# Squared-ReLU activations of two transformer layers: rectified in place, squared two tiles at a time, with a new table of pace settings

## The chip, the cores and the metric

The kernel runs on one core of a Trainium2 chip. A core has five engines that work side by side and are synchronised by semaphores: TensorE (PE; matmuls, results in the PSUM banks), VectorE (DVE), ScalarE (ACT; here nearly only exponentials), GpSimd (POOL) and SyncE (SP; here it issues DMAs). The metric is the device time of one execution in microseconds (us), as the median of several runs; lower is better.

## What is computed

Two transformer layers on 2048 rows of 448 numbers (bfloat16), with the same weights: attention of 16 heads (28 wide) and a feed-forward network (FFN) with 1792 hidden units, whose activation is a squared ReLU.

```python
def _A_ref(x, wqkv, wo):                      # attention
    ...
    scores = jnp.einsum("bhqd,bhkd->bhqk", q, k) * scale
    p = _softmax(scores, axis=-1)
    o = jnp.einsum("bhqk,bhkd->bhqd", p, v)
    return (lambda x, *d: x.transpose(*d))(o, 0, 2, 1, 3).reshape(B, S, D) @ wo

def _B_ref(x, w1, b1, w2, b2):                # FFN
    h = jnp.einsum("bsd,df->bsf", x, w1) + b1
    zero = jnp.zeros_like(h)
    r = jnp.where(h > zero, h, zero)
    h = r * r
    out = jnp.einsum("bsf,fd->bsd", h, w2) + b2
    return out

x = A_x
x = x + _A_ref(_layernorm(x, axis=-1), A_wqkv, A_wo)
x = x + _B_ref(_layernorm(x, axis=-1), B_w1, B_b1, B_w2, B_b2)
x = x + _A_ref(_layernorm(x, axis=-1), A_wqkv, A_wo)
x = x + _B_ref(_layernorm(x, axis=-1), B_w1, B_b1, B_w2, B_b2)
```

## The kernel before

**Tiling.** Everything stays in SBUF between the layers. The rows go in blocks of 256 (`nt` = 2 tiles of 128): eight in layer 0; seven in layer 1, and then two of 128 rows. Heads are held in four groups `g` of four heads, each head padded to 32 rows, so that four heads fill 128 partitions. One *score tile* is 512 columns of transposed scores in one PSUM bank: for a block of 256 rows, one head and two tiles of keys. There are 1024 of them in each layer.

**The order is written at build time.** A planner (`Planner`, `run`) simulates the engines' clocks with a cost for each operation and lays down, one operation after the other, what each engine's instruction queue holds. Streams of operations compete by start time and by priority; the chip then executes the queues in that order. So a cost or a setting in the planner acts only through the order and the choices that it makes.

**Groups.** `s_stream` issues the score matmuls in groups of three score tiles (line 1154); `gi` is the number of the group, 683 in all. ScalarE turns a group into exponentials with one instruction (line 1192). ScalarE's share of a group can be cut to two tiles: then `apart` has picked a third tile for VectorE, and `a_unit` (line 1216 or 1214) and its followers compute its exponential there with integer arithmetic on the bits, sharing steps with GpSimd (`a_rest`, lines 1263 to 1278) or on VectorE alone (`a_whole`, lines 1232 to 1239; chosen when GpSimd's backlog is over `PLIM`). `apart` allows a tile when VectorE's load over the last `SPAN` us is at most `BUSY` (or `LOW`, when the FFN work is behind its track) and its backlog at most `TB` (or `TB2`). Groups listed in `FORCE` get a tile without these two tests, groups in `SKIP` get none.

**Pace.** The settings are module variables, and `PACE` maps a group's number to settings that hold from that group on (`globals().update(PACE.get(gi, {}))`).

**The values.** `p_stream` multiplies the exponentials with V (lines 1380 and 1345), `CHUNK` key tiles at a time. Then come normalisation, the output projection and the layer norm.

**The FFN** of a block is made in `chain`: the matmuls with `w1` (`mm_tile`, line 809) fill a PSUM tile of 512 columns, which is two chunks of 128 hidden units for a block of 256 rows, so seven tiles a block; for a block of 128 rows four chunks and four tiles. VectorE rectifies each tile into a buffer `r` (line 1584; two such buffers, `R_r`), and squares it from there into its place (line 1591), which `hidden` finds: parts of `K_sb[1]`, `Q_sb` and `V_sb[1]` that are no longer needed, and a tile `h`, in layer 0; `V_sb[0]` in layer 1. When the score groups are at an end, ScalarE takes some of these (lines 1582, 1589). Products with `w2` follow, and wait for the block's last square. `add_to_x` adds the result to `x_sb` (line 1513).

**Fillers.** To keep TensorE occupied, `s_stream` may repeat a group's score matmuls (up to `MORE` times), and `heat` puts in products whose result isn't used, when TensorE's load over `WINDOW` is below `HEAT`.

Of the kernel before, what the change touches and what calls it, by code (L numbers as in the profile page):

```python
# [38 lines left out]
XMIN = 4  # L39
HELD = 0.14  # L40
# [42 lines left out]
HTURNS = 3  # L83
C_PRIO = 1.6
# [65 lines left out]
PACE = {  # L150
    0: {'BUSY': 0.95, 'LOW': 0.7, 'CHUNK': 1, 'EV': 2.9, 'FAR': 6, 'KEEP': 5, 'LAG': 8, 'LEAD': 18, 'MARGIN': 3,
         'MORE': 3, 'PRE': 0.5, 'SLACK': 0.7, 'SPAN': 8, 'TB': 2.4, 'TB2': 2.4, 'V_AGE': 5, 'V_LAST': 3, 'V_PAST':
         2, 'C_PRIO': 1.6, 'V_PRIO': 4, 'V_LATE': 2.6, 'V_WAIT': 5, 'ASIDE': 1, 'XMIN': 4, 'HOLD': 6, 'LADD': 0.05,
         'RES': 2, 'RES2': 2, 'TASIDE': -0.2, 'EPRIO': 2.6, 'SPARE': 0, 'NEAR': 3, 'SOON': 1, 'VGAP': 0.03, 'PWAIT':
         0.3, 'PNEAR': 0.2, 'PORTP': 1, 'PLIM': 99.0},
    8: {'LEAD': 12, 'BUSY': 0.9, 'PLIM': 2},
    16: {'SPAN': 11},
    24: {'LAG': 3},
    32: {'PLIM': 2.6, 'EV': 3.5},
    40: {'TB2': 3.0},  # L160
    42: {'BUSY': 0.95, 'CHUNK': 3, 'EV': 2.9, 'LAG': 8, 'LEAD': 18, 'MORE': 1, 'SPAN': 8, 'TB': 1.6, 'TB2': 2.4,
         'V_PRIO': 8.5},
    56: {'BUSY': 1.0, 'LAG': 3},
    64: {'NEAR': 9, 'ASIDE': 0.2, 'LADD': 0.1},
    72: {'V_AGE': 4},
    88: {'V_AGE': 3},
    112: {'C_PRIO': 1.2, 'HOLD': 5},
    120: {'LEAD': 10, 'LAG': 12, 'SPARE': 3, 'ASIDE': 2},
    128: {'TB': 2.0, 'MORE': 3},
    136: {'PRE': 1.2, 'MARGIN': 6},  # L170
    144: {'EPRIO': 4},
    152: {'CHUNK': 1, 'VGAP': 0},
    160: {'BUSY': 0.95, 'V_PRIO': 4, 'V_PAST': 3},
    168: {'RES': 1, 'C_PRIO': 2.1, 'LOW': 1.0},
    176: {'EV': 2.2, 'TB2': 2.0, 'LOW': 0.5},
    192: {'PORTP': 0.3, 'SOON': 0.6},
    200: {'CHUNK': 2, 'PRE': 0.3},
    208: {'PNEAR': 0.25, 'V_AGE': 6},
    216: {'NEAR': 3},
    248: {'EPRIO': 6},  # L180
    256: {'ASIDE': 0},
    264: {'MARGIN': 10},
    280: {'PORTP': 2},
    288: {'HOLD': 6},
    296: {'TB': 1.0, 'PNEAR': 0.15},
    304: {'SPAN': 6},
    312: {'BUSY': 1.0},
    320: {'LEAD': 12, 'MARGIN': 6},
    328: {'V_LATE': 6},
    336: {'LOW': 1.0},  # L190
    360: {'PNEAR': 0.05, 'TB': 2.4, 'V_LATE': 2.6, 'V_AGE': 3},
    368: {'C_PRIO': 1.6},
    376: {'PNEAR': 0.15, 'V_PRIO': 8.5},
    384: {'XMIN': 3, 'LEAD': 18},
    392: {'CHUNK': 3},
    400: {'KEEP': 6, 'ASIDE': 4, 'V_AGE': 6, 'BUSY': 0.9},
    408: {'PWAIT': 0.6, 'MORE': 1},
    424: {'RES': 2, 'BUSY': 1.0},
    440: {'HEAT': 0.6, 'WINDOW': 3.4, 'CHUNK': 2},
    456: {'V_AGE': 5, 'TB': 1.3},  # L200
    480: {'TB': 1.6, 'PORTP': 0.3, 'PLIM': 2},
    488: {'LADD': 0.2, 'HOLD': 4},
    496: {'MARGIN': 3, 'PNEAR': 0.35},
    504: {'PWAIT': 0.3},
    512: {'KEEP': 4, 'EV': 2.9},
    520: {'V_AGE': 4, 'C_PRIO': 1.2, 'HOLD': 5},
    528: {'PRE': 0.8},
    536: {'XMIN': 4, 'SPAN': 15, 'ASIDE': 2, 'PRE': 0.3},
    544: {'V_AGE': 5, 'EV': 2.2},
    552: {'PORTP': 1, 'LEAD': 12, 'FAR': 17, 'PRE': 0},  # L210
    560: {'V_LATE': 6, 'VGAP': 0.03},
    568: {'SPARE': 0, 'NEAR': 9},
    576: {'SOON': 1.5, 'PNEAR': 0.15},
    584: {'PLIM': 1.3, 'LAG': 3, 'V_WAIT': 3},
    592: {'KEEP': 6, 'V_LAST': 2.2},
    600: {'V_AGE': 8},
    608: {'EV': 1.3, 'LOW': 0.8},
    616: {'PRE': 1.2, 'BUSY': 0.95, 'V_PAST': 2, 'FAR': 6},
    624: {'LADD': 0.1, 'BUSY': 0.9},
    648: {'PRE': 0.5, 'SPAN': 20, 'EV': 3.5, 'ASIDE': 0.2},  # L220
    656: {'ASIDE': 1, 'SLACK': 0.4},
    672: {'SOON': 1, 'ASIDE': 0.2},
    680: {'SLACK': 0.7},
# [183 lines left out]
def kernel(  # L407
# [45 lines left out]
    R_r, R_xt, R_os, R_xn, R_on, R_rec = Res(2), Res(2), Res(NOS), Res(2), Res(2), Res(2)  # L453
# [31 lines left out]
    def flat_of(t):  # L485
        return t[:, :, :].rearrange("p g s -> p (g s)")
# [63 lines left out]
    def loads():  # L550
# [28 lines left out]
        yield dma(b2w[0:1, :], B_b2.rearrange("(o d) -> o d", o=1), 30 * kb, ("b2",))  # L579
# [937 lines left out]
    def chain(l, qb):  # L1517
# [30 lines left out]
        if late:  # L1548
            b2b = flat_of(K_sb[0])[:, S:S + D]
            if ("b2b",) not in pl.tok:  # L1550
# [11 lines left out]
        def hidden(i):  # L1562
            flat = lambda a: a.rearrange("p (f q) -> p f q", q=n)
            if l == 0 and i < 4:
                return (K_sb[1], Q_sb)[i // 2][:, 2 * (i % 2):2 * (i % 2) + 2, t0 * P:t0 * P + n]
            if l == 0 and i < 6:
                return flat(V_sb[1][:, t0:t0 + nt, :, :].rearrange("p t h r -> p (t h r)")[:, QB * (i - 4):QB * (i - 3)])
# [4 lines left out]
            return flat(V_sb[0][:, :, :, :].rearrange("p t h r -> p (t h r)")[:, c:c + QB])  # L1572
        for f0 in range(0, NFC, pack):
            fcs = range(f0, min(f0 + pack, NFC))
            w = len(fcs) * n
            split = late > 2 - THALF and f0 == 0
            b = {}

            def relu(e, t, b=b, w=w):
                r = b["r"] = rp.tile([P, QB], DT.bfloat16, name="r")  # L1580
                if e == "ACT":
                    nc.scalar.activation(out=r[:, 0:w], in_=t[:, 0:w], func=AF.Relu)  # L1582
                else:
                    nc.vector.tensor_scalar(out=r[:, 0:w], in0=t[:, 0:w], scalar1=0.0, scalar2=None, op0=ALU.max)  # L1584
            def square(e, b=b, w=w, f0=f0):
                r = b["r"][:, 0:w].rearrange("p (f q) -> p f q", q=n)
                b["h"] = h = hidden(f0 // pack)
                if e == "ACT":
                    nc.scalar.activation(out=h[:, 0:w // n, :], in_=r, func=AF.Square)
                else:  # L1590
                    nc.vector.tensor_tensor(out=h[:, 0:w // n, :], in0=r, in1=r, op=ALU.mult)  # L1591

            def then(o, b=b, square=square):
# [3 lines left out]
            o = yield from mm_tile(  # L1597
                [(i * n, n, [(w1[:, dc, fc * P:(fc + 1) * P], xnT[:, dc, 0:n], *([ends[dc // 2]] if split else [])) for dc in range(NDC)])
                 for i, fc in enumerate(fcs)],
                relu, 0.685, [*([] if split else ends), ("w1",)], True, post=[then], acq=R_r, across=split)  # L1600
            done[l] += w / 512
            for i in range(len(fcs)):
                hacts.append((b, i, b["s"]))
        yield Op("DVE", 0.0, None, deps=[o], rel=own_xt)
        mv = moments()
        for j in range(nt):
# [21 lines left out]
    def heat():  # L1628


        for gi in itertools.count(HFROM):
# [3 lines left out]
            for turn in range(HTURNS):  # L1635
                if HEAT <= pl.load(WINDOW) or not s_left or len(units) - at[0] < HSTOP:
                    break
# [57 lines left out]
```

## Time and profile before

| | us |
|---|---|
| median of 3 runs (803.57 to 803.78) | 803.65 |
| the profiled execution's own time | 803.48 |
| its span, from the first to the last instruction | 801.7 |

A row of the page's fifth part reads: line, engine, operation, output and inputs with shapes, count | busy us, mean ns of one | idle time of the engine before them, and what ended most of it. A row of stretches reads: start and end, length, then the busy us of each engine with its count of instructions, the granted TensorE clock, the DMA share and GB/s. Matmul ends are modelled, and a busy PE is not PE at its peak.

### The profile page before, as it was taken

Reading aid. Unit: us, or ns where it says so; the run is one execution under the profiler, and the core shown is the slowest. Engines: PE = TensorE matmul, PEld = TensorE weight load, DVE = VectorE, ACT = ScalarE, POOL = GpSimd, SP = SyncE. Lnnn points to the kernel's source line nnn. Section 1 sums busy time; section 2 is a strip of 40 time slices with the busy share of each in tenths; the row PEclk is TensorE's granted clock in tenths of the full one; section 3 lists DMA queues with packets and bytes.
Section 4 is the critical chain, followed back from the end, with each engine's and each line's share of the span. In section 5 each row is a group of like instructions: output and inputs, shape, how many; then the busy total and the mean of one; then the engine's idle time right before and its main releaser. Section 6 shows DMA issues by size and latency. Waiting matters only on the chain.

```text
span 801.7 us, 29246 instructions
## 1 busy us (share of the span) xinstructions
PE 778.7 (97%) x12242; PEld 417.6 (52%) x12242; DVE 744.8 (93%) x1818; ACT 789.4 (98%) x702; POOL 454.7 (57%) x717
## 2 busy tenths in 40 slices
PE   9999989999999999999999999989999999999998
PEld 6555545544555545555455545445454544545666
DVE  8999999999999999999999998999999999989564
ACT  8999999999999999999999999999999999999995
POOL 3346777657676664544566657657665566654200
PEclk9999999999999999999999999999999999999999
DMA  9300010000000000000000000011100000000100
GB/s 250 86 2 2 5 34 23 17 16 16 17 3 16 16 16 16 3 16 15 2 3 2 3 2 2 15 32 30 33 11 22 21 28 21 22 23 9 27 8 19
DMA packets 32480, 18.13 MB, mean 23 GB/s; under 512 B 17818, under 2 KB 31899, under 8 KB 32348
## 3 DMA queue, kind: packets, MB, share of 16 engines
q1 hardware_dynamic: 32204, 16.16, 7.4%
q8 instruction: 95, 1.56, 0.8%
q14 instruction: 37, 0.30, 0.1%
q10 hardware_dynamic: 144, 0.11, 0.0%
HBM read 13.98 MB, written 2.06 MB: 20 GB/s over the span
## 4 chain that ended last, share of the span: by engine, by line
PE 41%; ACT 33%; DVE 17%; issue 8%; DMA 0%; POOL 0%; ACTq 0%; DVEq 0%
ACT pt L1192 33%; PE mt L809 19%; PE sc L1154 12%; PE oT L1380 7%; DVE pt L1216 2%; DVE r L1584 2%; PE oT L1345 1%; DVE pt L1214 1%; DVE V_sb L1591 1%; DVE K_sb L1278 1%; DVE v_c L1278 1%; DVE v_c L1216 1%; PE tp L712 1%; DVE x_sb L1513 1%; PE sc L809 1%
## 5 line engine op out<-in xcount | busy, mean ns | idle before, releaser
L1192 ACT ACTIVATE pt<-sc 128x1536 bf16<-128x1536 f32 (+1 forms) x683 | 776.6, 1292 | 1.2 <-PE sc L1154 0.9
L1154 PE MATMUL sc<-Q_sb,K_sb 32*128 32x256 bf16 (+1 forms) x4652 | 279.6, 265 | 15.7 <-ACT pt L1192 13.5
L1154 PEld LDWEIGHTS <-K_sb 32*128 32x128 bf16 x4652 | 101.1, 92 | 186.3 <-issue 118.3
L1380 PE MATMUL oT<-pt,V_sb 128*32 128x256 bf16 (+1 forms) x4000 | 167.8, 268 | 0.5 <-DVE Q_sb L828 0.3
L1380 PEld LDWEIGHTS <-V_sb 128*32 128x32 bf16 x4352 | 101.5, 96 | 45.3 <-issue 35.9
L809 PE MATMUL mt<-xnT,w 128*128 128x256 bf16 (+1 forms) x904 | 119.6, 270 | 0.9 <-DVE xnT L724 0.2
L1274 POOL TENSOR_SCALAR pt<-pt 128x512 int16<-128x512 int8 x131 | 83.9, 642 | 39.9 <-ACT pt L1192 5.7
L809 PEld LDWEIGHTS <-w 128*128 128x128 bf16 x952 | 78.0, 98 | 35.2 <-issue 26.4
L1216 DVE TENSOR_SCALAR pt<-sc 128x512 int16<-128x512 f32 x132 | 89.8, 684 | 2.3 <-PE sc L1154 1.6
L1584 DVE TENSOR_SCALAR r<-mt 128x512 bf16<-128x512 f32 (+1 forms) x107 | 73.0, 682 | 3.8 <-PE mt L809 3.4
L673 POOL TENSOR_TENSOR rstd<-mv,mhalf 128x2 f32<-128x2 f32 (+1 forms) x34 | 25.4, 747 | 76.4 <-DVE mv L676 48.2
L809 PE MATMUL mt<-w,V_sb 128*128 128x448 bf16 (+2 forms) x288 | 66.5, 345 | 0.0
L1274 POOL TENSOR_SCALAR v_c<-v_c 128x512 int16<-128x512 int8 x64 | 42.8, 668 | 24.5 <-DVE V_sb L1269 4.3
L1269 POOL TENSOR_SCALAR v_c<-pt 128x512 f16<-128x512 uint8 x57 | 37.8, 663 | 31.9 <-DVE K_sb L1263 5.8
L1513 DVE TENSOR_TENSOR x_sb<-x_sb,mt 128x448 bf16<-128x448 bf16 x61 | 37.4, 612 | 12.9 <-PE mt L809 12.6
L1216 DVE TENSOR_SCALAR v_c<-sc 128x512 int16<-128x512 f32 x69 | 46.6, 682 | 0.7 <-PE sc L1154 0.6
L648 DVE BATCH_NORM_STATS2 st<-x_sb 128x6 f32<-128x448 bf16 x63 | 38.9, 619 | 0.7 <-DMA x_sb<-in_A_x_dram 0.5
L809 PEld LDWEIGHTS <-V_sb 128*128 128x128 bf16 x302 | 25.4, 98 | 24.4 <-issue 10.0
L1345 PE MATMUL oT<-v_c,V_sb 128*32 128x256 bf16 (+1 forms) x298 | 35.0, 273 | 0.0
L1591 DVE TENSOR_TENSOR V_sb<-r 128x512 bf16<-128x512 bf16 x70 | 29.2, 421 | 3.0 <-ACT r L1582 2.8
L1274 POOL TENSOR_SCALAR K_sb<-K_sb 128x512 int16<-128x512 int8 x39 | 25.3, 650 | 11.2 <-DVE v_c L1278 2.4
L1269 POOL TENSOR_SCALAR K_sb<-pt 128x512 f16<-128x512 uint8 x35 | 23.9, 682 | 13.2 <-DVE pt L1216 4.3
(219 smaller groups left out, 1254.0 us busy)
## 6 DMA issues: line engine op xcount, KB each, us to landing
rec<-scr SPq DMA_DIRECT2D x54, 128.0 KB
out_dram<-x_sb SPq DMA_DIRECT2D x15, 112.0 KB
x_sb<-in_A_x_dram SPq DMA_DIRECT2D x7, 224.0 KB
w<-in_B_w_dram SPq DMA_DIRECT2D x1, 1568.0 KB
w<-in_B_w_dram SPq DMA_DIRECT2D x1, 1344.0 KB
dn<-oT_sb SPq DMA_DIRECT2D x54, 4.0 KB
V_sb<-in_A_wqkv_dram SPq DMA_DIRECT2D x4, 168.0 KB
scr<-dn SPq DMA_DIRECT2D x27, 8.0 KB
```

What stands on the lines that cost most here:

```text
L648: nc.vector.bn_stats(out=box["st"][:, :], in_=x_sb[:, t0 + j, :] if src is None else src())
L809: nc.tensor.matmul(box["t"][:, c0:c0 + n], lhsT=lhsT() if callable(lhsT) else lhsT, rhs=rhs, start=a, stop=b)
L1154: nc.tensor.matmul(dst[k][:, i * nt * P:(i + 1) * nt * P], lhsT=K_sb[l][rows, g, (kb + i) * P:(kb + i + 1) * P], rhs=Q_sb[rows, g, t0 * P: ...
L1192: t = nc.scalar.activation(out=pt[:, 0:n], in_=gbuf[gi]["sc"][:, 0:n], func=AF.Exp, scale=float(np.log(2.0)) * 2.0 ** -FRAC)
L1216: t = nc.vector.tensor_scalar(out=z.bitcast(DT.int16), in0=src, scalar1=2.0, scalar2=EXP_BIAS, op0=ALU.mult, op1=ALU.add)
L1269: on(e).tensor_scalar(out=box["f"], in0=gbuf[gi]["z"].bitcast(DT.uint8).rearrange("p (n t) -> p n t", t=2)[:, :, 0], scalar1=2.0 ** -9, sc ...
L1274: on(e).tensor_scalar(out=gbuf[gi]["z"].bitcast(DT.int16), in0=gbuf[gi]["z"].bitcast(DT.int8).rearrange("p (n t) -> p n t", t=2)[:, :, 1], ...
L1345: nc.tensor.matmul(box["t"][DHP * hh:DHP * hh + DHP, 0:n], lhsT=V_sb[l][:, kb + i, 4 * g + hh, :], rhs=gbuf[gi]["x2"][:, i * n:(i + 1) * n ...
L1380: nc.tensor.matmul(box["t"][DHP * hh:DHP * hh + DHP, 0:n], lhsT=V_sb[l][:, tb, 4 * g + hh, :], rhs=p, start=begin and j < G, stop=close an ...
L1513: nc.vector.tensor_tensor(out=x_sb[:, tb, lo:hi], in0=x_sb[:, tb, lo:hi] if src is None else src[:, lo:hi], in1=t[:, 0:hi - lo], op=ALU.add)
L1584: nc.vector.tensor_scalar(out=r[:, 0:w], in0=t[:, 0:w], scalar1=0.0, scalar2=None, op0=ALU.max)
L1591: nc.vector.tensor_tensor(out=h[:, 0:w // n, :], in0=r, in1=r, op=ALU.mult)
```

## The change

Three things are done. First, in `chain` the rectifier writes straight into the place of the square, and the square is taken there, in place. Second, with `TWO` = 1, blocks of 256 rows square their tiles in pairs: tiles 0 and 1, 2 and 3, 4 and 5 with one instruction of 1024 columns each, and tile 6 alone; `hidden(i, 2)` hands out the place of two tiles. The buffers `r` and their resource `R_r` fall away, so a PSUM bank comes free when its tile is rectified, as before, and a rectifier no longer waits for a buffer. The planner's cost of a square becomes 0.153 + 0.267 for each 512 columns (0.42 before). Third, `PACE`, `FORCE` and `SKIP` are replaced as a whole. `HEAT` 0.6 with `WINDOW` 3.4 from group 440 on is no longer an entry of `PACE` but set by `HGAP`, `HEAT2` and `WINDOW2`. A variant with `b2` added on GpSimd comes with it, switched off (`BIAS` = 0).

```diff
+TWO = 1
...
-FORCE = (22, 27, 31, 36, 64, 104, 108, 120, 122, 156, 162, 192, 196, 233, 235, 237, 254, 263, 287, 292, 301, 306,
-         329, 341, 392, 408, 430, 445, 466, 501, 515, 553, 556, 567, 577, 593, 598, 602)
-SKIP = (20, 29, 46, 135, 184, 195, 216, 222, 242, 262, 280, 282, 320, 321, 378, 388, 395, 404, 406, 409, 416, 418,
-        433, 440, 446, 479, 500, 512, 526, 544, 574, 601, 609, 621, 622, 646, 652, 663)
+FORCE = (7, 27, 33, 52, 98, 119, 153, 194, 223, 248, 272, 292, 324, 363, 375, 394, 436, 438, 446, 451, 495, 532,
+         536, 552, 560, 637, 639, 645)
+SKIP = (14, 17, 23, 32, 37, 47, 111, 150, 159, 168, 178, 202, 203, 213, 251, 267, 353, 377, 378, 430, 452, 471, 479,
+        628)
 PACE = {
...
-    8: {'LEAD': 12, 'BUSY': 0.9, 'PLIM': 2},
-    16: {'SPAN': 11},
-    32: {'PLIM': 2.6, 'EV': 3.5},
...
-    56: {'BUSY': 1.0, 'LAG': 3},
-    128: {'TB': 2.0, 'MORE': 3},
-    160: {'BUSY': 0.95, 'V_PRIO': 4, 'V_PAST': 3},
-    312: {'BUSY': 1.0},
-    400: {'KEEP': 6, 'ASIDE': 4, 'V_AGE': 6, 'BUSY': 0.9},
-    408: {'PWAIT': 0.6, 'MORE': 1},
-    424: {'RES': 2, 'BUSY': 1.0},
-    616: {'PRE': 1.2, 'BUSY': 0.95, 'V_PAST': 2, 'FAR': 6},
-    624: {'LADD': 0.1, 'BUSY': 0.9},
...
+    8: {'PLIM': 2},
+    42: {'MORE': 1, 'TB': 1.6, 'V_PRIO': 8.5, 'EPRIO': 2.6, 'SPARE': 0},
+    160: {'SPAN': 15},
+    264: {'PLIM': 99},
+    312: {'V_LAST': 3.5, 'PLIM': 4},
+    352: {'LOW': 0.9, 'PLIM': 2.6},
+    408: {'PLIM': 2},
+    504: {'BUSY': 1.0},
...
-        def hidden(i):
+        def hidden(i, m=1):
...
-                return (K_sb[1], Q_sb)[i // 2][:, 2 * (i % 2):2 * (i % 2) + 2, t0 * P:t0 * P + n]
+                return (K_sb[1], Q_sb)[i // 2][:, 2 * (i % 2):2 * (i % 2) + 2 * m, t0 * P:t0 * P + n]
...
+            second = TWO and nt == 2 and i0 % 2 == 1
+            lone = not TWO or nt != 2 or f0 + pack >= NFC
+            if not second:
+                b = {"n": 0}
+            b["n"] += len(fcs)
...
-                r = b["r"] = rp.tile([P, QB], DT.bfloat16, name="r")
+                if not second:
+                    b["h"] = hidden(i0, 2 - lone)
+                k = w // n
+                h = b["h"][:, second * pack:second * pack + k, :]
+                src = t[:, 0:w].rearrange("p (f q) -> p f q", q=n)
...
-                    nc.vector.tensor_scalar(out=r[:, 0:w], in0=t[:, 0:w], scalar1=0.0, scalar2=None, op0=ALU.max)
+                    nc.vector.tensor_scalar(out=h, in0=src, scalar1=0.0, scalar2=None, op0=ALU.max)
...
+                h = b["h"][:, 0:b["n"], :]
...
-                    nc.vector.tensor_tensor(out=h[:, 0:w // n, :], in0=r, in1=r, op=ALU.mult)
+                    nc.vector.tensor_tensor(out=h, in0=h, in1=h, op=ALU.mult)
...
-                b["s"] = Op("ACT" if aside else "DVE", 0.5 if aside else 0.42, square, deps=[o], rel=o, port=True)
+                if not second:
+                    b["o"] = o
+                    if not lone:
+                        return []
+                b["s"] = Op("ACT" if aside else "DVE", 0.5 if aside else 0.153 + 0.267 * b["n"] * n / QB, square, deps=[b["o"], o], port=True)
                 return [b["s"]]
```

More of the change, by code (lines that the diff above doesn't have):

```diff
@@ L39 @@
 XMIN = 4
+BIAS = 0
+BDUR = 0.97
+BPRIO = 4.5
+TWO = 1
 HELD = 0.14
@@ L83 @@
 HTURNS = 3
+HGAP = (440, 10 ** 6)
+HEAT2 = 0.6
+WINDOW2 = 3.4
 C_PRIO = 1.6
@@ new lines @@
+    104: {'SLACK': 0.7},
+    112: {'V_PRIO': 6},
+    128: {'PORTP': 0},
+    136: {'MARGIN': 6},
+    160: {'SPAN': 15},
+    176: {'TASIDE': 0, 'V_AGE': 4},
+    192: {'TASIDE': -0.2},
+    208: {'HOLD': 5},
+    216: {'SOON': 0.6},
+    232: {'V_AGE': 3},
+    248: {'PORTP': 0.3},
+    264: {'PLIM': 99},
+    272: {'LAG': 16},
+    280: {'TASIDE': 0.2},
+    288: {'KEEP': 6},
+    312: {'V_LAST': 3.5, 'PLIM': 4},
+    336: {'LADD': 0.2},
+    344: {'V_LAST': 3},
+    352: {'LOW': 0.9, 'PLIM': 2.6},
@@ new lines @@
+    384: {'XMIN': 3, 'LADD': 0.1},
+    392: {'C_PRIO': 1.2},
+    408: {'PLIM': 2},
+    440: {'NEAR': 6, 'LAG': 8},
+    448: {'V_PAST': 3},
+    456: {'LAG': 12},
+    472: {'VGAP': 0},
+    480: {'C_PRIO': 2.1},
+    488: {'SOON': 1},
+    504: {'BUSY': 1.0},
+    520: {'V_PAST': 0, 'ASIDE': 0.2},
+    528: {'XMIN': 4},
+    544: {'EPRIO': 6},
+    552: {'SPARE': 1},
+    592: {'V_LAST': 3.5, 'RES2': 6},
+    600: {'LAG': 3, 'HOLD': 6},
+    608: {'V_PAST': 5, 'LEAD': 12, 'SOON': 1.5},
+    616: {'PNEAR': 0.15, 'V_LATE': 6},
@@ L224 @@
+    624: {'EV': 1.3},
+    632: {'KEEP': 4},
+    640: {'MARGIN': 10},
+    664: {'PRE': 0, 'LAG': 5},
 }
@@ L1548, in chain @@
         if late:
-            b2b = flat_of(K_sb[0])[:, S:S + D]
-            if ("b2b",) not in pl.tok:
+            b2b = b2w[:, :] if BIAS else flat_of(K_sb[0])[:, S:S + D]
+            if not BIAS and ("b2b",) not in pl.tok:
                 yield dma(b2b, B_b2.rearrange("(o d) -> o d", o=1).to_broadcast([P, D]), 112 * 1024, ("b2b",))
@@ L1594, in then @@
+            def then(o, b=b, square=square, lone=lone, second=second):
                 aside = not s_left and (l, qb) == (1, len(blocks[1]) - 2)
-                b["s"] = Op("ACT" if aside else "DVE", 0.5 if aside else 0.42, square, deps=[o], rel=o, port=True)
+                if not second:
[3 more added lines that the diff above has]
+                b["s"] = Op("ACT" if aside else "DVE", 0.5 if aside else 0.153 + 0.267 * b["n"] * n / QB, square, deps=[b["o"], o], port=True)
@@ L1599, in chain @@
                  for i, fc in enumerate(fcs)],
-                relu, 0.685, [*([] if split else ends), ("w1",)], True, post=[then], acq=R_r, across=split)
+                relu, 0.685, [*([] if split else ends), ("w1",)], True, post=[then], across=split)
             done[l] += w / 512
             for i in range(len(fcs)):
-                hacts.append((b, i, b["s"]))
+                hacts.append((b, i + second * pack))
         yield Op("DVE", 0.0, None, deps=[o], rel=own_xt)
@@ L1635, in heat @@
             for turn in range(HTURNS):
-                if HEAT <= pl.load(WINDOW) or not s_left or len(units) - at[0] < HSTOP:
+                least, span = (HEAT2, WINDOW2) if HGAP[0] <= gi < HGAP[1] else (HEAT, WINDOW)
+                if least <= pl.load(span) or not s_left or len(units) - at[0] < HSTOP:
                     break
```

100 lines of the change are left out of this document (25 added, 75 removed).

## The prediction

> **What bounds the kernel now.** I read the page's busy shares first, then the exponentials by form, then stretches of the program, then the squares. The first view gives every engine's busy time over the span.
>
> ```profile
> span 801.7 us, 29246 instructions
> PE 778.7 (97%) x12242; PEld 417.6 (52%) x12242; DVE 744.8 (93%) x1818; ACT 789.4 (98%) x702; POOL 454.7 (57%) x717
> PEclk9999999999999999999999999999999999999999
> L1192 ACT ACTIVATE pt<-sc 128x1536 bf16<-128x1536 f32 (+1 forms) x683 | 776.6, 1292 | 1.2 <-PE sc L1154 0.9
> ```
>
> ScalarE is busy 98% of the span and its 683 exponentials (line 1192) sat idle for 1.2 us in all. So the time is the sum of ScalarE's exponentials plus a start and a tail that the exponentials don't fill. TensorE's 97% isn't a second wall: part of it is filler, as shown below. The groups of ScalarE by form say what its sum is made of.
>
> ```profile
> L1192 ACT ACTIVATE pt<-sc 128x1536 bf16<-128x1536 f32 x345 | 490.1, 1504 | 0.6 <-PE sc L1154 0.5
> L1192 ACT ACTIVATE pt<-sc 128x1024 bf16<-128x1024 f32 x338 | 338.4, 1076 | 0.6 <-PE sc L1154 0.4
> ```
>
> There are 2048 score tiles of 512 columns (1024 in layer 0 and 1024 in layer 1, from the loop over passes), always three to a group: 345 groups leave all three to ScalarE, 338 leave two, and there VectorE takes the third with integer arithmetic (lines 1214, 1216), save in the last group, which has only two. So 337 tiles go to VectorE. One tile moved saves ScalarE 1504 - 1076 = 428 ns. That is the exchange rate of the whole kernel: any VectorE time set free is worth something only as tiles moved off ScalarE, and any VectorE time lost costs the same.
>
> The stretches tell how full VectorE is, beside which pace setting. The columns are length, then busy time of PE, weight loads, DVE, ACT and POOL.
>
> ```profile
> 20.00:750.00 730.00, 712.14 (x11049) 372.33 (x11048) 702.79 (x1697) 729.38 (x649) 445.07 (x698) 1.00 0.06 17
> 76.00:194.00 118.00, 112.76 (x1754) 59.53 (x1750) 114.70 (x273) 118.00 (x108) 82.31 (x128) 1.00 0.07 18
> 194.00:366.00 172.00, 170.52 (x2545) 90.17 (x2547) 162.13 (x386) 171.87 (x151) 99.29 (x160) 1.00 0.05 14
> 366.00:465.00 99.00, 96.70 (x1521) 51.33 (x1514) 97.55 (x243) 98.84 (x90) 59.51 (x95) 1.00 0.01 4
> 492.00:582.00 90.00, 83.97 (x1321) 42.05 (x1320) 89.05 (x218) 90.00 (x84) 59.90 (x94) 1.00 0.10 25
> 706.00:750.00 44.00, 43.27 (x828) 24.32 (x827) 39.30 (x96) 44.00 (x39) 20.70 (x32) 1.00 0.05 15
> ```
>
> Between 20 and 750 us VectorE idles 730 - 702.79 = 27.2 us, and ScalarE 0.6 us. The share follows the BUSY setting, the load above which the planner gives VectorE no further tile. By counting exponentials, the second to sixth rows hold about groups 56 to 164, 164 to 315, 315 to 405, 429 to 513 and 626 to 665. With BUSY 1.0 VectorE is at 97.2% (114.70 / 118), 98.5% and 98.9%; with 0.95 (third row) at 94.3%; with 0.9 (last row) at 89.3%. The setting is obeyed, and that is what lets me price a new table of settings at all.
>
> **The squares.** Each row gives a form of the squares or of an operation that I compare them with.
>
> ```profile
> L1591 DVE TENSOR_TENSOR V_sb<-r x70: 284/419/595, 143.8 to 796.9; 128x512 bf16<-128x512 bf16 x69, 128x256 bf16<-128x256 bf16 x1
> L1591 DVE TENSOR_TENSOR K_sb<-r x16: 386/418/501, 130.7 to 457.4; 128x512 bf16<-128x512 bf16 x16
> L1591 DVE TENSOR_TENSOR Q_sb<-r x16: 406/418/791, 133.8 to 461.3; 128x512 bf16<-128x512 bf16 x16
> L1591 DVE TENSOR_TENSOR h<-r x8: 387/419/608, 151.6 to 468.0; 128x512 bf16<-128x512 bf16 x8
> L724 DVE COPY xnT<-tp 128x1024 bf16<-128x1024 bf16 x26 | 17.7, 679 | 0.4 <-PE tp L712 0.3
> L724 DVE COPY xnT<-tp 128x512 bf16<-128x512 bf16 x3 | 1.3, 423 | 0.5 <-PE tp L712 0.5
> ```
>
> A block of 256 rows has seven hidden tiles of 512 columns. Before, seven squares; after, three double ones and a lone one. Fifteen blocks are of that kind, so 15 x 3 = 45 squares disappear into others; the two last blocks of 128 rows keep theirs. A square of 1024 columns isn't in the trace. The nearest row is the copy of bf16: 679 ns for 1024 columns against 423 for 512, so 256 ns for the second half. A double square should last about 420 + 256 = 676 ns, against 2 x 420 = 840: 164 ns less. But durations overlap at their ends, as the order of time on VectorE shows (start, duration, instruction):
>
> ```profile
> 133.44 0.42 DVE L1591 TENSOR_TENSOR K_sb<-r 128x512 bf16<-128x512 bf16 x1
> 133.78 0.42 DVE L1591 TENSOR_TENSOR Q_sb<-r 128x512 bf16<-128x512 bf16 x1
> 134.11 0.69 DVE L1216 TENSOR_SCALAR pt<-sc 128x512 int16<-128x512 f32 x1
> ```
>
> Two squares that last 0.42 us each start 0.34 and 0.33 us before what follows: the engine is taken for 0.335, and 0.085 of each is hidden under its neighbour. A pair takes 0.67, a double one 0.676 - 0.085 = 0.59. The saving is 0.08 us a pair, 45 x 0.08 = 3.5 us of VectorE. Bounds: nothing, if the second half costs as much as a square of its own (0.335), and 45 x 0.164 = 7.4 us if none of the overlap remained. I take 3.5, since in the row above the squares do overlap.
>
> Here the Trainium skill speaks of a larger price: "VectorE: DVE Perf Modes", section "Side-by-side: where the cycles go for N=2048 bf16", counts about 150 cycles of init and decode in every instruction. At the 0.96 GHz that the page gives, 45 instructions fewer would by that be about 7 us, and the time lower by a further 1.4 us or so. The trace agrees with the duration, 420 ns being 256 for the columns and 164 besides, and not with the cost: 85 of the 164 lie under the neighbour.
>
> What does a moved tile cost VectorE? The rows of the operations of such a tile:
>
> ```profile
> L1216 DVE TENSOR_SCALAR pt<-sc 128x512 int16<-128x512 f32 x132 | 89.8, 684 | 2.3 <-PE sc L1154 1.6 <-issue 0.2
> L1278 DVE TENSOR_TENSOR v_c<-v_c 128x512 bf16<-128x512 bf16 x63 | 26.4, 419 | 1.1 <-POOL v_c L1269 1.1
> L1239 DVE TENSOR_SCALAR pt<-pt 128x512 int16<-128x512 int16 x31 | 9.7, 317 | 0.2
> L1263 DVE TENSOR_SCALAR v_c<-pt 128x512 int16<-128x512 int16 x21 | 6.0, 286 | 0.0
> L1263 POOL TENSOR_SCALAR v_c<-pt 128x512 int16<-128x512 int16 x30 | 19.9, 663 | 11.9 <-DVE pt L1216 6.2 <-DVE oTn L1504 2.6 <-DVE K_sb L1236 1.0
> ...
> L1214 DVE TENSOR_SCALAR pt<-sc x31: 674/684/694, 56.9 to 724.9; 128x512 int16<-128x512 f32 x31
> L1214 DVE TENSOR_SCALAR K_sb<-sc x12: 676/686/695, 178.9 to 666.7; 128x512 int16<-128x512 f32 x12
> L1214 DVE TENSOR_SCALAR V_sb<-sc x11: 671/683/691, 95.2 to 718.1; 128x512 int16<-128x512 f32 x11
> L1214 DVE TENSOR_SCALAR v_c<-sc x10: 676/688/695, 71.6 to 523.6; 128x512 int16<-128x512 f32 x10
> L1214 DVE TENSOR_SCALAR h<-sc x3: 680/681/687, 500.9 to 596.8; 128x512 int16<-128x512 f32 x3
> ```
>
> Less 0.085 of overlap each: 0.60 for the first step and 0.335 for the closing product, always; 0.20 for line 1263 where VectorE does it and not GpSimd (21 against 30 of the commonest form; I take half). That is about 1.05 us. A tile done on VectorE alone (lines 1214, 1232, 1236, 1239; the five forms of line 1214 make 67 of 337) takes 0.60 + 0.20 + 0.335 + 0.20 = 1.34. The mean is (270 x 1.05 + 67 x 1.34) / 337 = 1.11 us. So 3.5 us are 3.2 tiles, 3.2 x 0.428 = **1.3 us off the time**; by the bounds 0 to 7.4 / 1.11 x 0.428 = 2.9 us.
>
> **The rest of the rewrite** I cost at nothing, for these reasons. The rectifier writes strided bf16 into Q_sb, K_sb or V_sb in place of r; it reads PSUM at 685 ns (line 1584), and the evacuations of the same size into Q_sb and K_sb are as long:
>
> ```profile
> L1584 DVE TENSOR_SCALAR r<-mt 128x512 bf16<-128x512 f32 x106 | 72.6, 685 | 3.8 <-PE mt L809 3.4
> L828 DVE TENSOR_SCALAR Q_sb<-mt 128x512 bf16<-128x512 f32 x30 | 20.5, 684 | 3.6 <-PE mt L809 3.4
> ```
>
> A square in place reads one operand twice as before. The first square of a pair now waits for the second rectifier, but the products with w2 wait for the last square of the block anyway, which is the lone seventh and comes as before. The two buffers of r no longer hold a rectifier back; in the row its idle time is 3.4 of 3.8 us for TensorE, so nothing is gained there. The rectifier now needs the place of its square free one instruction earlier; if it weren't, every later VectorE instruction would queue behind it, and ScalarE wouldn't get its scores' bank back. Line 1591 shows no wait for such a place now, so that is zero. GpSimd, kept off while VectorE holds the port, is held up to 0.34 us longer 45 times; it idles 730 - 445 = 285 us in the long row above.
>
> **The pace.** The new table changes who gets tiles. By its BUSY entries: 0.95 up to group 504, then 1.0 to the end (before 1.0 in groups 56 to 160, 312 to 400 and 424 to 616, and 0.95 or 0.9 from 616). Late: 706 to 750 us rises from 89.3% to the 98.9% of the rows with 1.0, 44 x 0.096 = 4.2 us, 3.8 tiles, **1.6 us off**. Middle: three rows may fall to 94.3%: 118 x 0.029 + 99 x 0.042 + 90 x 0.046 = 11.7 us, 10.5 tiles, up to 4.5 us more; at best 0, if the longer averaging (SPAN 15 for 8 from group 160) and the deeper allowed backlog keep VectorE as full. I take **1.7 more**, below the middle. Forced groups beyond the skipped ones: 28 - 24 = 4, before 38 - 38 = 0: between 0 and 4 tiles; I take all, **1.7 off**, as both tables are exceptions to the same rule.
>
> Sum: -1.3 - 1.6 + 1.7 - 1.7 = -2.9 us. The profiled execution took 803.48 us, 1.8 beside its span of 801.7, and 0.17 under the median of 803.65. From the median: **800.7 us**. A change under 0.2% (1.6 us) can't be told from none on this kernel.
>
> **Rivals.**
> *The table finds much more.* Half of the 27.2 us of idle VectorE is filled: 13.6 / 1.11 x 0.428 = 5.2, with the squares 6.5: 797.1 us. For it: ScalarE has no idle time to hide the gain. Against: some of those gaps are waits of VectorE for TensorE that no setting removes. Chance 0.16.
>
> *Nothing comes through.* VectorE's saved time becomes idle time, because the new caps bind exactly there: 803.6 us. For it: rows with a lower cap do stand idle while ScalarE is full. Chance 0.15.
>
> *The caps bind in the middle (slower).* One mechanism: between 76 and 582 us VectorE is held at 94 to 95%, the forced groups only stand for groups that the rule would have taken, and late there is no room, TensorE being at 43.27 of 44. Price 4.5 - 1.3 = 3.2: 806.8 us. It decides when fewer than 337 - 4 = 333 tiles go to VectorE, since each costs 0.428 and 1.6 us make a difference. For it: the shares obeyed the cap in every row. Against: the forced list. Chance 0.23.
>
> *TensorE loses its filler.* The new table leaves MORE at 1 where it was 3 in groups 128 to 408; the trace has score matmuls beyond need:
>
> ```profile
> L1154 PE MATMUL sc<-Q_sb,K_sb 32*128 32x256 bf16 x4080 | 261.3, 272 | 15.6 <-ACT pt L1192 13.5 <-DVE st L648 0.3
> L1641 PE MATMUL mt<-xn,ident 128*128 128x448 bf16 x30 | 9.9, 357 | 0.1
> ```
>
> 4080 of 256 columns against 3840 needed (the 1920 tiles of the blocks of 256 rows, two matmuls each), so 240 repeats, and 30 idle products. They are slack for TensorE, which is why I call it no wall: 240 x 261.3 / 4080 = 15 us, and 9.9. If fewer of them let the clock fall, TensorE would become the bound; a clock of 0.9 over groups 128 to 408 (about 310 us at 97 to 99% busy) would be 310 x 0.11 = 34 us less those 25 of slack: 9 us more, 812 us. The granted clock is 1.00 in every row above, where TensorE is busy 93% and more. Chance 0.04. (The Trainium skill, "TensorE: Matmul & The Clock Gate", section "Part 1: The HAM clock gate (the "warmup" mystery)", has the clock halved after an idle window of some 3.4 us; no row here shows such a window.)
>
> **How the numbers follow.** The forecast has chance 0.42. Faster by over 0.2%: 0.42 + 0.16 = 0.58; within: 0.15; slower: 0.23 + 0.04 = 0.27. The forecast's own range is 800.7 less 1.6 + 1.7 (squares and middle at their best) and plus 2.8 (middle at its worst): 797.4 to 803.5. The range to hold 8 in 10 reaches to both larger rivals: 796 to 807 us.
>
> **What would show it.** Squares: 65 VectorE squares for line 1591's 110, 45 of them 128x1024 at about 676 ns, and still some 0.085 under the neighbour. Tiles: more than 337 exponentials on VectorE (forecast 344: 3.2 + 3.8 - 4 + 4), so that the 1024-column form on ScalarE counts 345 and the 1536-column form 338. Late: DVE near 98% in the stretch before 750 us. Middle: shares between 94 and 98%. ScalarE's idle time before line 1192 stays near 1.2 us, the clock at 1.00. Wrong it would be if that idle time grew by several us (then order on TensorE sets the time and not the number of tiles), or if a double square took 840 ns.

## The result, and the profile after

The changed kernel takes 806.98 us (median of 6 runs, 806.54 to 807.45) against 803.64: 3.3 us slower, a ratio of 1.0041 with a 95% interval of 1.0031 to 1.0051. The profiled execution took 807.45 us, the longest of the six, with a span of 805.7. The page after the change begins so (busy us of each engine, then the exponentials, whose line is now 1176).

```profile
span 805.7 us, 29308 instructions
PE 779.9 (97%) x12283; PEld 418.5 (52%) x12283; DVE 750.1 (93%) x1757; ACT 789.2 (98%) x704; POOL 484.7 (60%) x753
L1176 ACT ACTIVATE pt<-sc 128x1536 bf16<-128x1536 f32 (+1 forms) x683 | 775.3, 1292 | 3.0 <-PE sc L1138 2.4
```

The groups of exponentials by form, and the squares:

```profile
L1176 ACT ACTIVATE pt<-sc 128x1536 bf16<-128x1536 f32 x342 | 490.1, 1506 | 2.5 <-PE sc L1138 2.2 <-ACT pt L1176 0.3
L1176 ACT ACTIVATE pt<-sc 128x1024 bf16<-128x1024 f32 x341 | 344.6, 1076 | 0.5 <-PE sc L1138 0.2
...
L1591 DVE TENSOR_TENSOR V_sb<-V_sb 128x1024 bf16<-128x1024 bf16 x29 | 20.2, 696 | 0.1
L1591 DVE TENSOR_TENSOR Q_sb<-Q_sb 128x1024 bf16<-128x1024 bf16 x8 | 5.5, 685 | 0.0
L1591 DVE TENSOR_TENSOR K_sb<-K_sb 128x1024 bf16<-128x1024 bf16 x8 | 5.4, 680 | 0.0
```

The change does what it says: 45 double squares at 680 to 696 ns. More tiles go to VectorE than before, not fewer (341 groups of two on ScalarE, before 338), and ScalarE's exponentials keep it busy 775.3 us, 1.3 less than before. Yet the program is longer. Where it went is seen in the order of time at the end of ScalarE's work (start, duration, instruction), first of the kernel before, then of the changed one:

```profile
784.50 2.59 ACT L1192 ACTIVATE pt<-sc 128x1536 bf16<-128x1536 f32 x2
```

```profile
782.71 5.13 ACT L1176 ACTIVATE pt<-sc 128x1536 bf16<-128x1536 f32 x4
```

The last exponential ends at 787.09 us before and at 787.84 after, 0.75 later. From there to the end of the span it is 14.6 us before and 17.9 after. So 3.25 of the 4.0 us of span are in the tail, where no exponential runs (the medians differ by 3.3 us, the two profiled executions by 0.7 more). The stretches of the two tails (length, then PE, weight loads, DVE, ACT, POOL busy, clock), before and after:

```profile
787.09:801.70 14.61, 11.51 (x153) 9.39 (x150) 6.45 (x18) 4.93 (x9) 1.67 (x2) 1.00 0.06 17
```

```profile
787.84:805.70 17.86, 13.03 (x175) 10.61 (x172) 7.80 (x19) 6.05 (x11) 2.62 (x3) 0.97 0.06 17
```

TensorE has 22 matmuls and 1.5 us more to do there, and idles 1.7 us more. The lower clock of 0.97 isn't the reason: a run below with the same 175 matmuls in its tail (single squares in the order of the changed kernel) shows 1.00 there, and 17.80 us. The 0.75 us ahead of it are 3 tiles x 0.428 = 1.3 us saved, against 1.8 us more idle time of ScalarE (3.0 for 1.2; 1.0 of it is one wait for scores at 501 us) and 0.2 us of later start (9.5 for 9.3 us).

Why is more of the FFN left for the tail? The 22 matmuls are products with `w1` of the two blocks of 128 rows: of their 112, 22 start before the last exponential ends in the kernel before, and none in the changed one. The last blocks reach their FFN later. These are VectorE's steps of the last block of 256 rows: addition of the attention's output, normalisation, copy of the transposed rows. Before:

```profile
736.18 0.62 DVE L1513 TENSOR_TENSOR x_sb<-x_sb,mt 128x448 bf16<-128x448 bf16 x1
...
743.21 0.40 DVE L772 TENSOR_SCALAR xn<-x_sb,mv,rstd 128x448 bf16<-128x448 bf16 x1
...
744.99 0.69 DVE L724 COPY xnT<-tp 128x1024 bf16<-128x1024 bf16 x1
```

After:

```profile
752.53 0.62 DVE L1497 TENSOR_TENSOR x_sb<-x_sb,mt 128x448 bf16<-128x448 bf16 x1
...
757.80 0.70 DVE L756 TENSOR_SCALAR xn<-x_sb,mv,rstd 128x448 bf16<-128x448 bf16 x2 [0.81 <-POOL rstd L657]
...
760.32 0.69 DVE L708 COPY xnT<-tp 128x1024 bf16<-128x1024 bf16 x1 [0.26 <-PE tp L696]
```

The rows are ready 15 us later, but not all of that is lost: in the kernel before TensorE is busy with the FFN of the block ahead until 757 us, so the block's first product with `w1` starts 4.5 us later (761.89 for 757.37 us), and its last FFN addition 0.7 us later (784.79 for 784.10). What falls behind the last exponential is the next block, the first of 128 rows. Its transposed rows are copied here before the change, and here after it:

```profile
769.77 0.42 DVE L724 COPY xnT<-tp 128x512 bf16<-128x512 bf16 x1
```

```profile
787.72 0.42 DVE L708 COPY xnT<-sc 128x512 bf16<-128x512 bf16 x1 [2.31 <-PE sc L696]
```

In the changed kernel these rows are normalised at 776.32 us and transposed by TensorE at 787.29 only, behind other work in its queue. So the order that the planner laid down for TensorE has a part in it; no run changed that order alone.

VectorE is fuller in the stretch ahead of this, with 42.56 of 44 us between 706 and 750 us, before 39.30:

```profile
706.00:750.00 44.00, 42.73 (x855) 23.84 (x855) 42.56 (x102) 43.20 (x40) 30.18 (x46) 1.00 0.05 14
```

Counted in the order of ScalarE's exponentials, 18 of the groups 624 to 665 have two tiles, before 13. That is the very gain that the prediction counted, and the experiments ask what it is worth.

### The profile page after: what moved, and what is told of

Same layout as the page of the kernel before. It is cut to its first block, busy times and chain, and to the rows that moved or that the text cites. A ratio compares the mean times of both kernels' runs of the same rounds, so it can differ in the third digit from the quotient of the medians.

```text
span 805.7 us, 29308 instructions
## 1 busy us (share of the span) xinstructions
PE 779.9 (97%) x12283; PEld 418.5 (52%) x12283; DVE 750.1 (93%) x1757; ACT 789.2 (98%) x704; POOL 484.7 (60%) x753
## 4 chain that ended last, share of the span: by engine, by line
ACT 45%; PE 34%; DVE 10%; issue 9%; DMA 1%; POOL 1%; SPq 0%; ACTq 0%; DVEq 0%; POOLq 0%
ACT pt L1176 45%; PE mt L793 14%; PE sc L1138 10%; PE oT L1364 6%; PE oT L1329 1%; DVE pt L1200 1%; PE sc L793 1%; PE tp L696 1%; DVE V_sb L1584 1%; DVE st L632 1%; DMA rec<-scr 0%; DVE pt L1198 0%; DVE v_c L1262 0%; DMA scr<-dn 0%; DVE xn L756 0%
## 5 line engine op out<-in xcount | busy, mean ns | idle before, releaser
L1176 ACT ACTIVATE pt<-sc 128x1536 bf16<-128x1536 f32 (+1 forms) x683 | 775.3, 1292 | 3.0 <-PE sc L1138 2.4
L1364 PE MATMUL oT<-pt,V_sb 128*32 128x256 bf16 (+1 forms) x3968 | 160.5, 268 | 0.4 <-DVE Q_sb L812 0.3
L1258 POOL TENSOR_SCALAR pt<-pt 128x512 int16<-128x512 int8 x123 | 80.6, 657 | 35.8 <-ACT pt L1176 6.6
L1200 DVE TENSOR_SCALAR pt<-sc 128x512 int16<-128x512 f32 x124 | 84.5, 683 | 3.3 <-PE sc L1138 2.4
L793 PE MATMUL mt<-w,V_sb 128*128 128x448 bf16 (+1 forms) x274 | 66.0, 349 | 0.0
L1258 POOL TENSOR_SCALAR v_c<-v_c 128x512 int16<-128x512 int8 x77 | 50.0, 649 | 17.4 <-DVE v_c L1262 2.2
L1200 DVE TENSOR_SCALAR v_c<-sc 128x512 int16<-128x512 f32 x78 | 53.1, 681 | 1.2 <-PE sc L1138 0.8
L1584 DVE TENSOR_SCALAR V_sb<-mt 128x512 bf16<-128x512 f32 x66 | 44.9, 680 | 4.0 <-PE mt L793 3.6
L1253 POOL TENSOR_SCALAR K_sb<-pt 128x512 f16<-128x512 uint8 x41 | 28.6, 697 | 16.8 <-DVE K_sb L1247 5.1
L1258 POOL TENSOR_SCALAR K_sb<-K_sb 128x512 int16<-128x512 int8 x45 | 29.5, 656 | 13.5 <-DVE v_c L1262 1.4
L1253 POOL TENSOR_SCALAR v_c<-v_c 128x512 f16<-128x512 uint8 x39 | 25.4, 652 | 18.7 <-DVE v_c L1247 4.5
```

What stands on the lines that cost most here:

```text
L793: nc.tensor.matmul(box["t"][:, c0:c0 + n], lhsT=lhsT() if callable(lhsT) else lhsT, rhs=rhs, start=a, stop=b)
L1176: t = nc.scalar.activation(out=pt[:, 0:n], in_=gbuf[gi]["sc"][:, 0:n], func=AF.Exp, scale=float(np.log(2.0)) * 2.0 ** -FRAC)
L1200: t = nc.vector.tensor_scalar(out=z.bitcast(DT.int16), in0=src, scalar1=2.0, scalar2=EXP_BIAS, op0=ALU.mult, op1=ALU.add)
L1253: on(e).tensor_scalar(out=box["f"], in0=gbuf[gi]["z"].bitcast(DT.uint8).rearrange("p (n t) -> p n t", t=2)[:, :, 0], scalar1=2.0 ** -9, sc ...
L1258: on(e).tensor_scalar(out=gbuf[gi]["z"].bitcast(DT.int16), in0=gbuf[gi]["z"].bitcast(DT.int8).rearrange("p (n t) -> p n t", t=2)[:, :, 1], ...
L1364: nc.tensor.matmul(box["t"][DHP * hh:DHP * hh + DHP, 0:n], lhsT=V_sb[l][:, tb, 4 * g + hh, :], rhs=p, start=begin and j < G, stop=close an ...
```

## The experiments

Five kernels were made to tell apart three causes: the rewrite of the squares, the number of tiles, and the tail. Four more look at the rest of the tail and at what the prediction assumed. "In its order" means that the planner laid down the same order as in the kernel named and only the instructions of one step differ.

**Rectified in place, squared singly, old table.** The squares and their order as before; only `r` falls away.

```diff
-TWO = 1
+TWO = 0
 FORCE, SKIP, PACE: those of the kernel before
```

> The new code with the old table and single squares: rectified in place, squared one tile at a time, 337 tiles on VectorE, the order of the engines as before. Theory (in-place work is free, as the prediction costed it): 803.6 us, within 0.4. Rival (the rectifier now waits for the place of its square, and ScalarE's bank with it): 805 us or more, with VectorE idle time ahead of the rectifier's line.

Measured: 803.74 us, ratio 1.0002 [0.9993, 1.0011]. Working in place costs nothing, as the prediction had it.

**Double squares in the order of before.** The first square of a pair is left out of the queue, the second does both; the rectifiers write into one place for the pair.

```diff
...
+                if paired and i0 % 2 == 0:
+                    return
+                h = pb["h"] if paired else b["h"][:, 0:b["n"], :]
...
                 nc.vector.tensor_tensor(out=h, in0=h, in1=h, op=ALU.mult)
```

> The kernel before with its order of work kept, but the squares of two tiles issued as one instruction of 1024 columns where the second square stood; still 337 tiles on VectorE. Theory A (the time that the doubles free on VectorE is worth something only if tiles are moved for it): VectorE busy about 3.5 us less, time 803.6 within 0.5. Theory B (VectorE's queue itself is in the way of the scores): up to 3.5 us faster, about 801 us. Theory C (a double square blocks VectorE for 0.68 us at a stretch and delays what is behind it): 805 us or more.

Measured: 804.87 us, ratio 1.0015 [1.0006, 1.0024]. VectorE is busy 742.7 us, against 745.3 with single squares in place: 2.6 us less, not 3.5, and the program isn't faster. It even lost 1.3 us, less than theory C asked for, more than theory A allowed. The tail is the same (14.6 us in both profiles), so the loss lies ahead of it. There ScalarE's exponentials, with the same groups, are busy 777.6 us for 776.7; which step loses it isn't shown. VectorE's time set free is worth nothing here by itself.

**Single squares in the order of the changed kernel.**

```diff
-                    nc.vector.tensor_tensor(out=h, in0=h, in1=h, op=ALU.mult)
+                    for k in range(0, b["n"], pack):
+                        part = h[:, k:min(k + pack, b["n"]), :]
+                        nc.vector.tensor_tensor(out=part, in0=part, in1=part, op=ALU.mult)
```

> The changed kernel with its order of work kept, but each double square issued as two single ones, one behind the other. Theory (the doubles help a little and are not why the change is slower): VectorE busy 3.5 us more, time between 807.0 and 810.5. Rival (the doubles are what costs): below 806.2.

Measured: 812.94 us, ratio 1.0116 [1.0102, 1.0130], 6.0 us above the changed kernel, and more than the 810.5 that the theory allowed. So in this order the doubles aren't why the change is slower; it counts on them. The tail is as in the changed kernel (17.80 us); the loss lies ahead of it. VectorE's busy time rose by 8.1 us (758.2 for 750.1), more than twice what 45 squares cost by the prediction. Squares of this kernel (durations min/median/max), and one pair of them in the order of time:

```profile
L1593 DVE TENSOR_TENSOR K_sb<-K_sb x16: 354/418/833, 132.7 to 463.7; 128x512 bf16<-128x512 bf16 x16
L1593 DVE TENSOR_TENSOR Q_sb<-Q_sb x16: 406/412/830, 143.2 to 466.7; 128x512 bf16<-128x512 bf16 x16
...
132.69 1.17 DVE L1593 TENSOR_TENSOR K_sb<-K_sb 128x512 bf16<-128x512 bf16 x2
```

The median is the old 0.42 us, but some take 0.83, and the trace shows beside what. In the pair above, an instruction of GpSimd starts at 132.96 us, between the two squares, and ends at 133.59; the second square starts at 133.03 and ends at 133.86. Of the 109 squares 26 last over 0.5 us, 10.2 us above 0.42 in all. Each of the 26 starts while an instruction of GpSimd is running and ends 0.26 to 0.28 us after it. So most of the 6.0 us may be this and not the missing doubles as such; that part wasn't measured alone.

**The kernel before, with a few tiles more near the end.**

```diff
-    624: {'LADD': 0.1, 'BUSY': 0.9},
+    624: {'LADD': 0.1},
```

> The kernel before, with BUSY left at 0.95 from group 624 on in place of 0.9, so that VectorE takes some tiles more near the end. Theory (late, TensorE's work sets the end: a tile moved off ScalarE there shortens the exponentials and puts as much FFN work behind the last of them): the last exponential ends 0.5 to 1.2 us earlier, the tail behind it grows by 2 us or more, time 804.5 to 806. Rival, the prediction's step: each tile more takes 0.43 us off, time 802.4 to 803.2.

Measured: 806.62 us, ratio 1.0037 [1.0023, 1.0050]. One setting of the old table makes the kernel as slow as the whole change, a little above the 806 that the theory allowed. ScalarE has 340 groups of two tiles and ends its exponentials earlier; the last stretch is the tail:

```profile
L1192 ACT ACTIVATE pt<-sc 128x1536 bf16<-128x1536 f32 x343 | 487.2, 1499 | 0.5 <-PE sc L1154 0.5
L1192 ACT ACTIVATE pt<-sc 128x1024 bf16<-128x1024 f32 x340 | 340.1, 1074 | 0.6 <-PE sc L1154 0.4
...
779.63 6.63 ACT L1192 ACTIVATE pt<-sc 128x1536 bf16<-128x1536 f32 x5
...
786.26:804.80 18.54, 13.54 (x179) 10.72 (x176) 7.49 (x18) 6.44 (x13) 1.56 (x2) 1.00 0.07 21
```

The exponentials end at 786.26, which is 0.83 us earlier, as two tiles more should give; the tail is 18.5 us, 3.9 longer, with 2.0 us more of TensorE's work in it. VectorE shows why. The last block of 256 rows is added to at the same time as before, but the normalisation comes 4 us later, and the copy of its transposed rows 9 us later:

```profile
736.88 0.61 DVE L1513 TENSOR_TENSOR x_sb<-x_sb,mt 128x448 bf16<-128x448 bf16 x1
...
747.50 0.77 DVE L772 TENSOR_SCALAR xn<-x_sb,mv,rstd 128x448 bf16<-128x448 bf16 x2
...
754.38 0.69 DVE L724 COPY xnT<-tp 128x1024 bf16<-128x1024 bf16 x1
```

VectorE works as hard from 735 to 745 us in both (9.96 us before, 9.91 here), and on more tiles here (five begun, before three). The block's first product with `w1` starts 3.0 us later (760.33 us), and again none of the 112 of the two blocks of 128 rows starts before the last exponential ends. The FFN that TensorE would have done beside the exponentials is done behind them.

**The reverse: the changed kernel with fewer late tiles.**

```diff
...
-FORCE = (..., 560, 637, 639, 645)
+FORCE = (..., 560, 645)
 SKIP: the same, and 632 to 643
```

> The changed kernel with the groups 632 to 643 added to the skipped ones (and 637, 639 taken from the forced ones): no tile goes to VectorE there, 336 in all instead of 340 or 341. Theory (late tiles on VectorE delay the last blocks' normalisation and so put TensorE's FFN work behind the last exponential): the last exponential ends 1.7 to 2.5 us later than in the changed kernel (787.84), the tail is 2 us or more shorter, time 806.5 to 807.5, no slower. Rival, the prediction's exchange rate: 4 or 5 tiles fewer are 1.7 to 2.1 us more, 808.7 to 809.1.

Measured: 806.76 us, ratio to the kernel before 1.0046 [1.0032, 1.0059], and so as fast as the changed kernel. The rival's 808.7 or more is out: 336 groups of two tiles, five fewer, cost nothing. Among the groups 624 to 665 there are now 13, as many as in the kernel before. The exponentials end later, and the tail gives it back:

```profile
L1175 ACT ACTIVATE pt<-sc 128x1024 bf16<-128x1024 f32 x336 | 339.8, 1079 | 0.5 <-PE sc L1137 0.4
...
779.07 10.43 ACT L1175 ACTIVATE pt<-sc 128x1536 bf16<-128x1536 f32 x8
...
789.50:804.50 15.00, 10.65 (x130) 7.80 (x127) 7.04 (x17) 2.87 (x7) 1.59 (x2) 1.00 0.05 16
```

They end at 789.50, 1.7 us later than in the changed kernel, and the tail is 15.0 us for 17.9; 48 of the 112 products with `w1` now start before the last exponential ends. Together with the experiment before it this shows the exchange from both sides: near the end, a tile moved to VectorE shortens the exponentials and lengthens the tail, by as much or more. But it doesn't bring back the 3.3 us. With as many late tiles as before, the new table is still as slow; its loss then lies ahead of the tail, where the exponentials end 2.4 us later than in the kernel before (busy 777.4 us for 776.6, idle 2.9 for 1.2).

**GpSimd's addition held back.** In the changed kernel's tail one normalisation took 1.17 us instead of 0.39, while GpSimd added `b2` to the same block. Here that addition waits until the normalisation is through.

```diff
...
                 nc.gpsimd.tensor_tensor(out=xf, in0=x_sb[:, t0, :], in1=b2b, op=ALU.add)
+                tc.add_manual_dep(pl.seen[0], xn_ops[-1].made[0].name, ...)
...
```

> The changed kernel, with GpSimd's addition for each of the two last blocks held back until VectorE has normalised the block's rows; all else in its order. Theory (0.78 us of the longer tail are VectorE's normalisation waiting for the port behind that addition): 806.2 us, within 0.4, and the normalisation takes 0.39 us again. Rival (the tail waits for something else): 807.0.

Measured: 806.75 us (806.34 to 807.94), ratio to the kernel before 1.0040 [1.0027, 1.0054]. The row in the changed kernel and in this one:

```profile
791.69 1.17 DVE L756 TENSOR_SCALAR xn<-x_sb,mv,rstd 128x448 bf16<-128x448 bf16 x1
```

```profile
791.51 0.40 DVE L758 TENSOR_SCALAR xn<-x_sb,mv,rstd 128x448 bf16<-128x448 bf16 x1
```

The stretched instruction is explained, and the profiled tail is shorter by 0.8 us. But the median fell by 0.2 only, within the spread of either kernel, and lies between the theory's and the rival's; so this part of the tail isn't shown in the time.

**No repeated score matmuls**, in the order of before.

```diff
-                for i in list(range(4)) * (again + 1):
+                for i in range(4):
```

> The kernel before with its order of work kept, without the second and later passes over a group's score matmuls (300 matmuls whose result is written twice). The prediction called them slack: 803.6 us within 0.6, clock 1.00, TensorE about 15 us less busy. Rival A (TensorE is the bound wherever it is 97 to 99% busy): 795 us or less. Rival B (the filler keeps the clock up): granted clock below 0.99 and 806 us or more.

Measured: 804.34 us, ratio 1.0008 [0.9999, 1.0017], clock 1.00. The repeats are slack, as the prediction said: without them the kernel isn't faster (the time is 0.1 us above the theory's range). The size was off: TensorE's busy time fell by 6.1 us (772.6), not 15; why the 300 matmuls cost so little isn't shown.

**One setting of the old table changed early.**

```diff
-    56: {'BUSY': 1.0, 'LAG': 3},
+    56: {'BUSY': 0.95, 'LAG': 3},
```

> The kernel before with one setting of its table changed: BUSY 0.95 in place of 1.0 from group 56 on (until the next entry for it, at 160, which is 0.95 in both). By the prediction's arithmetic (share of VectorE times length, over the price of a tile): 118 us x 0.029 / 1.11 x 0.428, 1.3 us more, 805 us. Theory now (a table fits one order of work only; a group that goes another way shifts all groups behind it against the forced and skipped lists): over 820 us, far fewer than 337 tiles on VectorE, and most of the loss behind group 160, where no setting differs.

Measured: 850.71 us, ratio 1.0584 [1.0565, 1.0603]. The same forms, and a stretch of the middle (ACT is the fourth busy time):

```profile
L1192 ACT ACTIVATE pt<-sc 128x1024 bf16<-128x1024 f32 x326 | 326.2, 1074 | 31.7 <-PE sc L1154 31.2
...
76.00:194.00 118.00, 110.85 (x1743) 58.64 (x1739) 113.37 (x269) 117.86 (x107) 81.18 (x125) 1.00 0.07 17
...
465.00:582.00 117.00, 103.05 (x1487) 55.19 (x1486) 102.35 (x247) 92.14 (x86) 64.16 (x104) 0.99 0.05 12
```

Where the setting differs, between 76 and 194 us, VectorE is at 96.1% and not at 94.3%, and next to nothing is lost. The largest part of the loss comes 300 us later, between 465 and 582 us, where ScalarE is busy 92 of 117 us and waits for scores, with the table the same again. The tail is longer too, 23.3 us. Twelve tiles fewer are only 5 us.

**The double squares planned with the old table.**

```diff
 TWO = 1
 FORCE, SKIP, PACE: those of the kernel before
```

> The new code with double squares, planned with the old table (PACE, FORCE, SKIP of before). By the prediction's arithmetic the squares alone are worth 1.3 us: 802.3. Theory now (a table fits one order of work; another cost of the squares makes another order): over 825 us, with fewer than 333 tiles on VectorE and ScalarE waiting for scores; so a new table was not to be done without.

Measured: 847.26 us (844.38 and 850.13), ratio 1.0542 [1.0509, 1.0575], 330 groups of two tiles; ScalarE idles 31.4 us ahead of its exponentials. The old table doesn't carry over to the doubles. A comparison of the rewrite alone with the old table would have told nothing of the rewrite.

No kernel that was run is faster than the one before.

## Why the prediction was wrong

It forecast 800.7 us, and 806.98 came. The time is close to the rival with 806.8, but not by its mechanism: that one needed fewer than 333 tiles on VectorE, and there were 340. That 806.98 lies inside the wide range of 796 to 807 is luck: the range reached that far for this rival.

*The bound.* "That is the exchange rate of the whole kernel: any VectorE time set free is worth something only as tiles moved off ScalarE" is the step that failed. The rate of 0.428 us holds for ScalarE's busy time, and for the end of the exponentials where I could see it (two tiles: 0.83 us). It doesn't hold for the program's end. I had read ScalarE's idle time of 1.2 us as proof that nothing else sets the time, and put the tail aside as a constant. The tail is where TensorE's unfinished FFN goes, and it went from 14.6 to 17.9 us. None of the signs that I named for being wrong watches it.

*Late: -1.6.* The tiles came, five more among the groups 624 to 665 where I had 3.8, and VectorE did rise, to 96.7% (42.56 of 44) where I had 98.9%. They were worth nothing: five tiles fewer there changed the time by 0.2 us, and two more in the kernel before cost 3.0 us. I had the reason in hand, in the slower rival: "late there is no room, TensorE being at 43.27 of 44", and used it only for tiles that wouldn't be moved, not for what a moved tile does to the FFN behind it.

*Squares: -1.3.* Duration right (676 ns, measured 680 to 696), time set free about right (3.5 us, measured 2.6), worth nothing in the old order (+1.3 us). In the new order they are needed: without them 6.0 us are lost, for 8.1 us more of VectorE. In these two fixed orders, slack that was given wasn't taken up, and slack that was taken away was paid for in good part.

*Middle +1.7, forced groups -1.7.* The shares didn't obey BUSY. With 0.95 the changed kernel has, in the stretches of the prediction:

```profile
76.00:194.00 118.00, 112.85 (x1720) 59.28 (x1722) 115.12 (x266) 118.00 (x107) 78.82 (x119) 1.00 0.07 17
194.00:366.00 172.00, 169.63 (x2629) 90.13 (x2631) 166.90 (x381) 171.76 (x154) 108.70 (x172) 1.00 0.06 15
366.00:465.00 99.00, 97.10 (x1459) 50.74 (x1455) 90.64 (x209) 98.72 (x86) 62.16 (x97) 1.00 0.01 2
```

That is 97.6, 97.0 and 91.6%, where I had reckoned with 94 to 98%, and with 94.3% for a setting of 0.95. The agreement that I read off the kernel before didn't carry over. By number, the groups of two tiles are seven more among 160 to 311, where BUSY is 0.95 in both tables, and eight fewer among 312 to 399. Ahead of group 616 there are 318 of them, before 322: four fewer, where the terms for squares, middle and forced groups together had 3.2 more. The two settings that were tried alone cost 3 and 47 us, against 1.3 us by this arithmetic for the second; a table of such settings can't be priced entry by entry.

*At nothing:* the work in place, the buffers and the filler came out as costed. What I costed at nothing and shouldn't have is the place of other work in the queues: the layer norm of a block that stands behind moved tiles on VectorE, and the FFN that waits for it on TensorE.

The two experiments on the late groups show that the exchange rate fails near the end. They don't show that the late tiles are what makes the new table slower, since with fewer of them it is as slow. For that run the account is an estimate from its trace. Without the late term the forecast would be 802.3 us, and 806.76 came. There are 336 groups of two tiles where 341 were forecast (2.2 us), ScalarE idles 1.7 us more than before, and the tail is 0.4 us longer, together 4.3 of the 4.5 us.

Which entries of the new table cost the tiles ahead of the end and the 1.7 to 1.8 us of ScalarE's idle time, and why the doubles cost 1.3 us in the old order, stays open. The sum of the changed kernel's tail is not fully divided either: 1.5 us are TensorE's work, and of its 1.7 us of idle time 0.8 fall to one stretched instruction.

## What to carry to other kernels

When an engine is busy 98% of the time, ask what lies behind its last instruction before counting its savings: work of another nearly full engine that was hidden beside it can move there. A table of settings that was tuned for one set of costs can be worth little for another; test an edit in the old order (same queue, one step changed), and don't price such a table by its entries. Time freed on an engine in a fixed order was worth nothing here until something was moved for it.

## What the runs showed beside this

A normalisation on VectorE of 0.39 us took 1.17 us while GpSimd's addition of 1.03 us ran, and 0.40 when the addition was held back. And issuing 45 squares of 1024 columns as 90 of 512, back to back, raised VectorE's busy time by 8.1 us, where the start-to-start times of before (0.335 us a square) had let me expect 3.5; 26 of them took longer, most 0.83 us, and each of these started beside a running instruction of GpSimd and ended some 0.27 us after it. Of the other 83 squares 12 started beside one too and weren't stretched, so it isn't so beside every instruction of GpSimd. No run held GpSimd back there.
